# Two 128-row loads of a gated linear-attention kernel issued as two 64-row halves each

## The chip, the cores and the metric

The kernel runs on one core of a Trainium2 chip. The metric is the device time of one execution in microseconds (us); several executions are given, and their median is used. The engines are named as in the profile: PE is TensorE (its matmuls), PEld its weight loads, DVE is VectorE, ACT is ScalarE, POOL is GpSimd and SP is SyncE, which here only issues DMAs. ACT issues DMAs as well. In the profile the DMA queue q1 holds what SP issues, and q10 what ACT issues.

## The reference

```python
def _A_ref(x, wqkv, wo):            # B = 1, S = 2048, D = 640, bfloat16
    B, S, D = x.shape
    H = 32; Dh = D // H             # 32 heads of 20
    qkv = (x @ wqkv).reshape(B, S, 3, H, Dh).transpose(2, 0, 3, 1, 4)
    q, k, v = qkv[0], qkv[1], qkv[2]
    phi = lambda t: jnp.where(t > 0, t + 1, jnp.exp(t)) + 1e-6
    pq, pk = phi(q), phi(k)
    kv = jnp.einsum("bhsd,bhse->bhde", pk, v)
    z = jnp.einsum("bhsd->bhd", pk)
    num = jnp.einsum("bhqd,bhde->bhqe", pq, kv)
    den = jnp.einsum("bhqd,bhd->bhq", pq, z)[..., None] + 1e-6
    return (num / den).transpose(0, 2, 1, 3).reshape(B, S, D) @ wo
# _B_ref: the same with B's weights
x = A_x
g = sigmoid((x * gate_w).sum(-1, keepdims=True))
return g * _A_ref(x, A_wqkv, A_wo) + (1 - g) * _B_ref(x, B_wqkv, B_wo)
```

Both branches read the same `x`; only the weights differ.

## The kernel before

The 2048 rows of `x` are 16 tiles of 128 rows, the 640 features are 5 chunks of 128. All operations go through a small scheduler of the program (`sch.op`): each operation names what it reads and writes by keys such as `("XN", 0)`, and the scheduler puts in semaphore waits. It does not reorder: every engine runs its operations in the order in which the program names them.

The part that the change touches is the front, the first few microseconds. `XN` holds rows of `x` as they lie in memory, `XT` holds `x` transposed, and `WKT` holds the K weights, chunk by chunk (A's chunk `c` has the key `("WKH", 0, c)`). Every DMA is made by the helper `dma` (line 315), which gives it a semaphore of its own. The order of the front is written out by hand:

- SP's queue: `load_xn` for tiles 0, 1, 2, 3 of `x` (128 rows of 1280 bytes, 160 KB each), then A's K weights chunk 4, then B's K weights (two DMAs), then 15 DMA transposes that bring `XT` for tiles 4 to 15, then all the other loads.
- ACT's queue: `load_wk` for A's K weights chunks 0, 1, 2, 3 (160 KB each), then the gate's weights (`GWR`). These stand behind an exponential of one element (line 428) that brings in ACT's function table, and ahead of ACT's first work on data.
- PE: `fill` runs matmuls of a constant into a bank that nobody reads; `turn(t)` transposes tile `t` of `x` on PE, five transposes of 128x128 against the identity `IDN` (line 487), which DVE and ACT then copy to `XT` (lines 501 and 499); `ks((t, c))` is the part of the K projection of tile `t` for chunk `c`, one 512-wide and one 128-wide matmul.

PE's order at the front is

```python
fill(4, 12, 256)        # line 1037: 12 matmuls, 256 wide
turn(0, early)
fill(4, 1, 128)
ks((0, 0))
turn(1, early)
ks((0, 1), (1, 0), (1, 1))
turn(2, late)
ks((0, 2), (1, 2), (2, 0), (2, 1), (2, 2))
```

and then the gate's weights (`GWR`), tile 3, the rest of the K projection of tiles 0 to 3 for A, the same tiles for B, and pairs of both for tiles 4 to 15. Behind that come the Q projections, the per-head sums, and the output, in all some 180 us in which PE hardly pauses.

Of the kernel before, what the change touches and what calls it, by code (L numbers as in the profile page):

```python
# [8 lines left out]
ACT = mybir.ActivationFunctionType  # L9
# [3 lines left out]
D = 640  # L13
# [4 lines left out]
NC = 5  # L18
# [202 lines left out]
def bass_gated_mix__linear_attn_block__linear_attn_block__prompt_kernel(  # L221
# [16 lines left out]
    wqkv = {"A": A_wqkv, "B": B_wqkv}  # L238
    wo = {"A": A_wo, "B": B_wo}
    BR = ("A", "B")  # L240

    with ExitStack() as es:
        E = es.enter_context

        def sb(name, shape, dtype=dt.bfloat16):
            return E(nc.sbuf_tensor(name, shape, dtype))
# [3 lines left out]
        IDN = sb("IDN", [128, 128])  # L250
        GWR = sb("GWR", [128, 128])
        XN = sb("XN", [128, NT, D])
        XT = sb("XT", [128, NC, S])
# [4 lines left out]
        WKT = sb("WKT", [128, NC, BLO + 512])  # L258
# [5 lines left out]
        PK = {X: PKT[:, i, :, :] for i, X in enumerate(BR)}  # L264
# [29 lines left out]
        def bank(i, lo, hi, p0=0, p1=128):  # L294
            o = 512 * (i % 2)
            return PP[i // 2][p0:p1, o + lo : o + hi]
# [4 lines left out]
        def new_sem(name):  # L301
            n_sem[0] += 1
            return E(nc.semaphore(name="d%d_%s" % (n_sem[0], name)))

        sch = _Sched()

        def dma(eng, name, o_ap, i_ap, reads=(), writes=(), transpose=False, noncontig=None):
            sem = new_sem(name)

            def fn(engobj):  # L310
                if noncontig is not None:
                    with nc.allow_non_contiguous_dma(reason=noncontig):
                        ins = engobj.dma_start(o_ap, i_ap, transpose=transpose)
                else:
                    ins = engobj.dma_start(o_ap, i_ap, transpose=transpose)
                return ins.then_inc(sem, 16)

            return sch.op(eng, fn, reads=reads, writes=writes, name=name, sem=sem, total=16)

        def mms(steps, reads=(), writes=(), name=""):  # L320


            def fn(pe):
                ins = None
                for o, l, r, st, sp, tp in steps:
                    ins = pe.matmul(o, l, r, start=st, stop=sp, tile_position=tp)  # L326
                return ins

            return sch.op("PE", fn, reads=reads, writes=writes, name=name)
# [5 lines left out]
        def act(fn, reads=(), writes=(), name=""):  # L335
            return sch.op("ACT", fn, reads=reads, writes=writes, name=name)

        def dve(fn, reads=(), writes=(), name=""):
            return sch.op("DVE", fn, reads=reads, writes=writes, name=name)
# [4 lines left out]
        xin = A_x[0]  # L344


        def load_xn(eng, t0, t1):
            dma(
                eng,
                "xn%d" % t0,  # L350
                XN[:, t0:t1, :],
                xin[128 * t0 : 128 * t1, :].rearrange("(t p) f -> p t f", p=128),
                writes=[("XN", t) for t in range(t0, t1)],
            )
# [32 lines left out]
        def wk(X, c, h):  # L387

            if X == "A":
                return WKT[:, c, 512:D] if h else WKT[:, c, 0:512]  # L390
            return WKT[:, c, BHI : BHI + 129] if h else WKT[:, c, BLO : BLO + 512]

        def wk_reads(X):

            return [("WKH", BR.index(X), c) for c in range(NC)] + ([("WKL", c) for c in range(NC)] if X == "B" else [])

        def load_wk(eng, X, c0, c1):
            w = wqkv[X][128 * c0 : 128 * c1, D : 2 * D].rearrange("(c p) f -> p c f", p=128)
            parts = ((0, 0, D, "WKH"),) if X == "A" else ((BLO, 0, 512, "WKL"), (BHI, 512, D, "WKH"))
            for o, lo, hi, key in parts:  # L400
                dma(
                    eng,
                    "wk%s%d" % (X, c0),
                    WKT[:, c0:c1, o : o + hi - lo],
                    w[:, :, lo:hi],
                    writes=[(key, c) if key == "WKL" else (key, BR.index(X), c) for c in range(c0, c1)],
                )
# [10 lines left out]
                fill=0.0,  # L418
            ),
            reads=[("ONE",)],  # L420
            writes=[("IDN",)],
        )
        pool(lambda e: e.memset(GWR[:, :], 0.0), writes=[("GWZ",)])
        for X in BR:
# [3 lines left out]
            lambda e: e.activation(SG[:, 2, 0:1], nc.const_aps.tensor(1.0, (128, 1), dt.float32), ACT.Exp),  # L428
            writes=[("SGE", 0)],
        )  # L430
        for t in range(4):
            load_xn("SP", t, t + 1)
            load_wk("ACT", "A", t, t + 1)

# [5 lines left out]
            reads=[("GWZ",)],  # L440
            writes=[("GWR",)],
# [3 lines left out]
        for b in range(1, NB):  # L445
            for c in range(NC):
# [5 lines left out]
                    writes=[("XT", t, c) for t in range(4 * b, 4 * b + 4)],  # L452
# [19 lines left out]
        def fill(bk, n, w=512):  # L472
            mms(
                [(bank(bk, 0, w), C1[:, 0:128], C1[:, 0:w], True, True, None)] * n,
                writes=[("PS", bk)],
                name="fill",
            )

        def turn(t, parts):
            for cs, bk in parts:  # L480
                n = len(cs)
                dst = bank(bk, 0, 64 * n).bitcast(dt.bfloat16)

                def tr(pe, dst=dst, cs=cs):
                    ins = None
                    for i, c in enumerate(cs):
                        ins = pe.transpose(  # L487
                            dst[:, 128 * i : 128 * i + 128],
                            XN[:, t, 128 * c : 128 * c + 128],
                            IDN[:, :],  # L490
                        )
                    return ins

                sch.op("PE", tr, reads=[("XN", t), ("IDN",)], writes=[("PS", bk)], name="tr%d" % t)
                o = XT[:, cs[0] : cs[0] + n, 128 * t : 128 * t + 128]
                i = dst.rearrange("p (c s) -> p c s", c=n)
                ks = [("XT", t, c) for c in cs]
                if cs[-1] == NC - 1:
                    act(lambda e, o=o, i=i: e.activation(o, i, ACT.Copy), reads=[("PS", bk)], writes=ks)
                else:  # L500
                    dve(lambda e, o=o, i=i: e.tensor_copy(o, i), reads=[("PS", bk)], writes=ks)  # L501
# [4 lines left out]
        def k_part(X, t, pp, cs, first, last):  # L506
            P = PP[pp]
            xs = slice(128 * t, 128 * t + 128)
            bks = [("PS", 2 * pp), ("PS", 2 * pp + 1)]
            for c in cs:  # L510
                l = XT[:, c, xs]
                st, sp = first and c == cs[0], last and c == cs[-1]
                mms(
                    [
                        (P[:, 0:512], l, wk(X, c, 0), st, sp, None),
                        (P[:, 512:D], l, wk(X, c, 1), st, sp, None),
                    ],
                    reads=[("XT", t, c), ("WKH", 0, c)],
                    writes=bks,
                    name="k%s%d" % (X, t),  # L520
                )
# [130 lines left out]
        def g_run(X, j, pp, units, out=()):  # L652


            P = PP[pp]
            steps = []
            for t, h in units:
                o, r = (
                    (P[:, 0:512], PK[X][:, t, 0:512]),
                    (P[:, 512:D], PK[X][:, t, 512:D]),  # L660
                    (P[:, 512 : D + 128].rearrange("p (i f) -> p i f", i=2), PKT[:, :, t, 512:D]),
                )[h]
                steps.append((o, XN[:, t, 128 * j : 128 * j + 128], r, t == 0, t == NT - 1, None))
            ts = sorted({t for t, h in units})
            two = any(u[1] == 2 for u in units)
            mms(
                steps,
                reads=[("XN", t) for t in ts] + [("PK", Y, t) for t in ts for Y in (BR if two else X)],
                writes=[("PS", 2 * pp + h) for h in (0, 1) if any((u[1] > 0) == h for u in units)],
                name="g%s%d" % (X, j),  # L670
            )
            for lo, hi, o, key in out:
                act(
                    lambda e, lo=lo, hi=hi, o=o: e.activation(o, P[:, lo:hi], ACT.Copy),  # L674
                    reads=[("PS", 2 * pp + h) for h in (0, 1) if (hi > 512 if h else lo < 512)],
                    writes=[(key, j)],
                )
# [352 lines left out]
        def ks(*units):  # L1030
# [3 lines left out]

        early = (((0,), 6), ((1, 2), 7), ((3, 4), 5))
        late = (((0, 1, 2), 6), ((3, 4), 7))
        fill(4, 12, 256)
        turn(0, early)
        fill(4, 1, 128)
        ks((0, 0))  # L1040
# [6 lines left out]
            reads=[("GWR",), ("GWZ",), ("IDN",)],  # L1047
            writes=[("PS", 7)],
            name="gw",
# [4 lines left out]
            reads=[("PS", 7)],  # L1054
            writes=[("GW",)],
# [76 lines left out]
        for i, fn in enumerate(late):  # L1132
            fn()
            if i % 4 == 3 and groups:
                X, b = groups.pop(0)
# [72 lines left out]
```

## Time and profile before

| what | value |
|---|---|
| median of 3 runs | 190.44 us (190.39 to 190.78) |
| the profiled execution | 190.54 us |
| its span, first to last instruction | 189.3 us |
| what lies around the span | 1.2 us |
| PE busy | 186.5 us, 99% of the span |
| DVE busy | 121.1 us, 64% |
| ACT busy | 69.2 us, 37% |
| DMA, mean over the span | 121 GB/s |

The span is the time from the first to the last instruction of one profiled execution; the time of that execution also has a start and an end that no instruction shows. Starts in the views are microseconds from the span's start. Matmuls are pipelined and their ends are modelled: of a row of matmuls the distance between starts tells the pace, not the length of one. Idle time is put in brackets behind an instruction, with what ended it.

### The profile page before, as it was taken

How to read it: one execution, taken by the hardware profiler on the slowest of the kernel's cores; microseconds unless marked ns; L12 is line 12 of the kernel's file. 1: busy time of each engine (PE TensorE's matmuls, PEld its weight loads, DVE VectorE, ACT ScalarE, POOL GpSimd, SP SyncE). 2: the span in 40 equal slices, each digit the busy share in tenths (PEclk: the TensorE clock that was granted, in tenths of full speed). 3: DMA queues.
4: the chain of work that ended last, by engine and by line, in shares of the span. 5: the costliest groups of instructions: out<-in, count | busy, mean ns of one | idle time of the engine just before them, and what ended most of it. 6: DMA issues, size and time to landing. Idle time of an engine off the chain costs nothing.

```text
span 189.3 us, 3423 instructions
## 1 busy us (share of the span) xinstructions
PE 186.5 (99%) x1310; PEld 101.4 (54%) x1310; DVE 121.1 (64%) x223; ACT 69.2 (37%) x137; POOL 45.7 (24%) x49
## 2 busy tenths in 40 slices
PE   8999999999999999999999999999999999999995
PEld 5655555555545455455455555744447555555554
DVE  1289999999997756565565665495035961976223
ACT  3276565666544442532532632270214500000000
POOL 2000323223244746635645543000000000000000
PEclk9999999999999999999999999999999999999999
DMA  5965459998493501261000003206586599321212
GB/s 180 342 128 88 100 97 187 359 281 178 143 282 44 5 0 13 90 146 38 0 3 3 0 2 101 74 3 166 178 249 186 170 228 311 114 84 55 73 69 69
DMA packets 38946, 22.91 MB, mean 121 GB/s; under 512 B 24090, under 2 KB 37394, under 8 KB 38930
## 3 DMA queue, kind: packets, MB, share of 16 engines
q1 hardware_dynamic: 36136, 19.62, 40.1%
q10 hardware_dynamic: 2794, 3.08, 5.4%
q8 instruction: 10, 0.16, 0.4%
q14 instruction: 6, 0.05, 0.1%
HBM read 16.78 MB, written 3.95 MB: 109 GB/s over the span
## 4 chain that ended last, share of the span: by engine, by line
PE 99%; DVE 0%; issue 0%
PE ps L326 98%; PE ps L487 1%; DVE OSTG L1010 0%
## 5 line engine op out<-in xcount | busy, mean ns | idle before, releaser
L694 POOL TENSOR_TENSOR ZS<-ZS,PKT 128x640 f32<-128x640 f32 x26 | 37.6, 1445 | 43.2 <-DVE PKT L602 20.6
L326 PE MATMUL ps<-PKT,XN 128*128 128x512 bf16 (+2 forms) x256 | 46.7, 332 | 0.0
L326 PE MATMUL ps<-WKT,XT 128*128 128x512 bf16 (+3 forms) x260 | 44.9, 334 | 0.0
L627 ACT ACTIVATE EQ<-ps 128x512 bf16<-128x512 f32 x40 | 23.9, 598 | 35.8 <-PE ps L326 35.4
L326 PEld LDWEIGHTS ps<-PKT,XN 128*128 128x128 bf16 x256 | 23.8, 98 | 21.6 <-ACT GT L674 0.2
L326 PEld LDWEIGHTS ps<-WKT,XT 128*128 128x128 bf16 x260 | 24.0, 99 | 19.6 <-DVE XT L501 0.3
L632 DVE TENSOR_SCALAR EQ<-EQ 128x512 bf16<-128x512 bf16 x40 | 15.0, 375 | 21.2 <-ACT EQ L627 20.4
L326 PE MATMUL ps<-WPA,PQA 128*128 128x512 bf16 (+4 forms) x165 | 26.3, 295 | 0.0
L326 PE MATMUL ps<-WPB,PQB 128*128 128x512 bf16 (+4 forms) x165 | 26.0, 295 | 0.0
L326 PE MATMUL ps<-XT,WQB 128*128 128x512 bf16 x100 | 23.2, 379 | 0.0
L326 PE MATMUL ps<-XT,WQA 128*128 128x512 bf16 x100 | 23.1, 379 | 0.0
L586 ACT ACTIVATE EK<-ps 128x512 bf16<-128x512 f32 (+1 forms) x36 | 18.4, 527 | 11.3 <-PE ps L326 9.9
L602 DVE SCALAR_TENSOR_TENSOR PKT<-ps,EK 128x512 bf16<-128x512 f32 (+1 forms) x36 | 21.7, 603 | 1.2
L326 PEld LDWEIGHTS ps<-WPA,PQA 128*128 128x128 bf16 x165 | 13.4, 98 | 9.4
L326 PEld LDWEIGHTS ps<-WPB,PQB 128*128 128x128 bf16 x165 | 13.3, 98 | 9.0
L1010 DVE CAST OSTG<-ps 128x640 bf16<-128x640 f32 (+2 forms) x13 | 9.6, 751 | 11.6 <-PE ps L326 11.6
L326 PEld LDWEIGHTS ps<-XT,WQB 128*128 128x128 bf16 x100 | 9.7, 98 | 10.6
L326 PEld LDWEIGHTS ps<-XT,WQA 128*128 128x128 bf16 x100 | 9.6, 98 | 10.7
L637 DVE SCALAR_TENSOR_TENSOR PQA<-ps,EQ 128x512 bf16<-128x512 f32 x20 | 13.8, 692 | 0.7
L637 DVE SCALAR_TENSOR_TENSOR PQB<-ps,EQ 128x512 bf16<-128x512 f32 x20 | 13.8, 692 | 0.7
L1012 ACT ACTIVATE OSTG<-ps 128x256 bf16<-128x256 f32 x1 | 0.4, 385 | 37.0 <-PE ps L326 37.0
L674 ACT ACTIVATE GT<-ps 128x640 bf16<-128x640 f32 (+1 forms) x10 | 6.5, 652 | 17.9 <-PE ps L326 17.9
(67 smaller groups left out, 105.5 us busy)
## 6 DMA issues: line engine op xcount, KB each, us to landing
out_dram<-OSTG SPq DMA_DIRECT2D x15, 160.0 KB, 1.8
XN<-in_A_x_dram SPq DMA_DIRECT2D x3, 640.0 KB, 7.8
WKT<-in_A_wo_dram SPq DMA_DIRECT2D x8, 160.0 KB, 4.5
PKT<-rsA SPq DMA_DIRECT2D x10, 128.0 KB, 3.4
XT<-rsB ACTq DMA_DIRECT2D x8, 128.0 KB, 5.6
WVA<-in_A_wqkv_dram SPq DMA_DIRECT2D x1, 800.0 KB, 9.9
WVB<-in_B_wqkv_dram SPq DMA_DIRECT2D x1, 800.0 KB, 5.4
XN<-in_A_x_dram SPq DMA_DIRECT2D x4, 160.0 KB, 3.3
```

The costliest lines, as they stand in the source:

```text
L326: ins = pe.matmul(o, l, r, start=st, stop=sp, tile_position=tp)
L487: ins = pe.transpose(dst[:, 128 * i : 128 * i + 128], XN[:, t, 128 * c : 128 * c + 128], IDN[:, :],)
L586: lambda e, ek=ek, ps=ps: e.activation(ek, ps, ACT.Exp),
L602: lambda e, o=o, v=v, ek=ek, ps=ps: e.scalar_tensor_tensor(out=o, in0=v(ps), scalar=0.0, in1=v(ek), op0=ALU.max, op1=ALU.add),
L627: lambda e: e.activation(EQ[:, slot, :], bank(bk, 0, 512), ACT.Exp),
L632: lambda e: e.tensor_scalar(EQ[:, slot, :], EQ[:, slot, :], 1.0, EPS, op0=ALU.min, op1=ALU.add),
L637: lambda e: e.scalar_tensor_tensor(out=PQ[X][:, k, cols], in0=bank(bk, 0, 512), scalar=0.0, in1=EQ[:, slot, :], op0=ALU.max, op1=ALU.add,),
L674: lambda e, lo=lo, hi=hi, o=o: e.activation(o, P[:, lo:hi], ACT.Copy),
L694: lambda e: e.tensor_tensor(out=ZS[:, :], in0=a, in1=b, op=ALU.add),
L1010: dve(lambda e, o=o, p=p: e.tensor_copy(o, p), reads=bks, writes=keys)
L1012: act(lambda e, o=o, p=p: e.activation(o, p, ACT.Copy), reads=bks, writes=keys)
```

## The change

Tile 0 of `x` and chunk 0 of A's K weights are each loaded by two DMAs of 64 rows instead of one of 128. The first 64 rows of each go through SP's queue, the others through ACT's queue; on both queues the half tile of `x` stands ahead of the half chunk of weights. Behind them SP loads tiles 1 to 3 of `x` as before and ACT chunks 1 to 3 of the weights. So each queue has one DMA more ahead of what follows. The first halves get keys of their own (`("XN", 0, "a")`, `("WKH", 0, 0, "a")`), and the readers of tile 0 and chunk 0 name both keys. At the front PE runs 10 instead of 12 of the 256-wide constant matmuls. The engines' orders are otherwise the same.

```diff
-        for t in range(4):
+        for o, src, key in (
+            (XN[:, 0, :], xin[0:128, :], ("XN", 0)),
+            (WKT[:, 0, 0:D], wqkv["A"][0:128, D : 2 * D], ("WKH", 0, 0)),
+        ):
+            for i, eng in enumerate(("SP", "ACT")):
+                r = slice(64 * i, 64 * i + 64)
+                dma(eng, "h%s%d" % (key[0], i), o[r, :], src[r, :], writes=[key] if i else [key + ("a",)])
+        for t in range(1, 4):
             load_xn("SP", t, t + 1)
             load_wk("ACT", "A", t, t + 1)
...
-                sch.op("PE", tr, reads=[("XN", t), ("IDN",)], writes=[("PS", bk)], name="tr%d" % t)
+                sch.op("PE", tr, reads=[("XN", t), ("XN", t, "a"), ("IDN",)], writes=[("PS", bk)], name="tr%d" % t)
...
-                    reads=[("XT", t, c), ("WKH", 0, c)],
+                    reads=[("XT", t, c), ("WKH", 0, c), ("WKH", 0, c, "a")],
...
-        fill(4, 12, 256)
+        fill(4, 10, 256)
```

More of the change, by code (lines that the diff above doesn't have):

```diff
@@ L393, in wk_reads @@
         def wk_reads(X):
-            return [("WKH", BR.index(X), c) for c in range(NC)] + ([("WKL", c) for c in range(NC)] if X == "B" else [])
+            return [("WKH", BR.index(X), c) for c in range(NC)] + [("WKH", 0, 0, "a")] + ([("WKL", c) for c in range(NC)] if X == "B" else [])
         def load_wk(eng, X, c0, c1):
@@ L667, in g_run @@
                 steps,
-                reads=[("XN", t) for t in ts] + [("PK", Y, t) for t in ts for Y in (BR if two else X)],
+                reads=[("XN", t) for t in ts] + [("XN", 0, "a")] + [("PK", Y, t) for t in ts for Y in (BR if two else X)],
                 writes=[("PS", 2 * pp + h) for h in (0, 1) if any((u[1] > 0) == h for u in units)],
```

## The prediction

> **What bounds the kernel now.** I read the page's busy times and chain first, then the front of the span as a timeline, then the DMAs of the same stretch by queue. The page says that PE is the bound from end to end:
>
> ```profile
> PE 186.5 (99%) x1310; PEld 101.4 (54%) x1310; DVE 121.1 (64%) x223; ACT 69.2 (37%) x137; POOL 45.7 (24%) x49
> ...
> PE 99%; DVE 0%; issue 0%
> ```
>
> So the change is worth what it moves in PE's stream at the front. The timeline of PE and its weight loads there:
>
> ```profile
> 0.84 2.72 PE L326 MATMUL ps<-const-bfloat16-1.0 128*128 128x256 bf16 x12 [0.84 <-PEq L1193]
> 3.58 0.45 PEld L487 LDWEIGHTS ps<-IDN,XN 128*128 128x128 bf16 x5 [0.50 <-DMA XN<-in_A_x_dram]
> 3.59 0.71 PE L487 MATMUL ps<-IDN,XN 128*128 128x128 bf16 x5
> 4.20 0.74 PE L326 MATMUL ps<-WKT,XT 128*128 128x512 bf16 x2
> 4.73 0.74 PE L487 MATMUL ps<-IDN,XN 128*128 128x128 bf16 x5
> 5.27 1.57 PE L326 MATMUL ps<-WKT,XT 128*128 128x512 bf16 x6
> 6.67 0.44 PE L487 MATMUL ps<-IDN,XN 128*128 128x128 bf16 x5
> 6.95 1.52 PE L326 MATMUL ps<-WKT,XT 128*128 128x512 bf16 x10
> ```
>
> Three things stand there. First, the real work begins at 3.59, when tile 0 of x has landed, and from then on every group begins where the one before it leaves the array. Second, the fills are over a little earlier: two that straddle 3.2 start at 2.93 and end (modelled) at 3.57, so they start 0.21 us apart, and twelve of them leave the array at 0.84 + 12 x 0.21 = 3.35. PE is short of work for about 0.24 us, no more. Third, the pace doubles inside the six matmuls at 5.27. A pair of 512 and 128 wide takes 4.73 - 4.20 = 0.53 us before them and (8.31 - 6.95)/5 = 0.27 us behind them (8.31 is where the next group begins). The six take 6.67 - 5.27 = 1.40 us; with n slow pairs, 0.53n + 0.27(3 - n) = 1.40, n = 2.2, and the step lies at about 6.45. The clock column of the profile reads 1.00 throughout and does not show this, so I go by the spacing. What PE does before 6.45 takes twice its time: work that starts d earlier there brings the end forward by d/2 only.
>
> Then the DMAs, between 2.55 and 2.90 and between 2.90 and 3.30:
>
> ```profile
> DMA packets 98, 0.13 MB, mean 358 GB/s; under 512 B 0, under 2 KB 98, under 8 KB 98
> ...
> q1 hardware_dynamic: 98, 0.13, 100.2%
> ```
>
> ```profile
> DMA packets 136, 0.15 MB, mean 384 GB/s; under 512 B 16, under 2 KB 136, under 8 KB 136
> ...
> q10 hardware_dynamic: 104, 0.13, 89.4%
> q1 hardware_dynamic: 32, 0.02, 16.0%
> ```
>
> Between 1.8 and 2.55 only 14 packets moved, all on q1. Then q1 alone has all 16 engines (tile 0 of x), then q10 has them (chunk 0 of the weights), then q1 again (tile 1). The two queues take turns, and x already goes first, at full rate. Its landing is 0.81 + 2.7 = 3.5.
>
> **The change part by part.** The sum is against the profiled execution, 190.54 us (span 189.3 and 1.2 around it), which lies 0.10 above the median of 190.44; at the end I take the 0.10 off.
>
> *Tile 0 in two halves.* It is the same 160 KB on the same 16 engines. At 384 GB/s that is 0.42 us, before as one turn of q1, now as half a turn of q1 and half a turn of q10. What precedes is a start, not a transfer: from the issue at 0.81 to 2.55 hardly anything moves. The halves are issued at 0.81 (SP) and 0.87 (ACT, where the weights' first DMA stands now), so both are in the queues long before 2.55. I take the landing unchanged at 3.5. Bounds: if q10 does not start as early as q1, the nearest row is its first packets at about 2.9, behind which half a tile needs 0.21 us, so tile 0 is whole some 0.15 us later; if the start-up is shared out and vanishes, the tile could come up to 2.55 - 1.84 = 0.7 us earlier (1.84: 0.81 plus the 1.03 us to the first packet). In PE's time that is +0.08 to -0.35 us; I take 0.
>
> A rule of the Trainium skill speaks against this part. DMA: Bandwidth & Descriptors, section Rules for kernel authors, says that two transfers to disjoint halves of the partitions share the same 16 engines, so splitting brings nothing and one transfer of 128 partitions is better. The full rate on q1 alone agrees with it; by the rule this term is 0 or a small loss, against the -0.35 of the other bound.
>
> *Ten fills instead of twelve.* They leave the array at 0.84 + 10 x 0.21 = 2.94, so 0.43 us of constant work goes. Nothing reads it, and tile 0 is not there yet: the idle time ahead of the transposes grows from 0.24 to 0.65 us. That costs 0, covered by the wait for tile 0. If that cover is gone, because the tile lands earlier, the fills' removal is what lets PE use it.
>
> *Two more DMA issues, and what they are moved past.* On SP the issues stand 0.46 us apart, so tiles 1, 2, 3, chunk 4, B's weights and the 15 transposes are all issued some 0.46 later. Tile 1 would be issued at 1.73 instead of 1.27; its data moved from about 3.3, and before that the queues are busy with tile 0 and chunk 0 in either version. It landed at 1.27 + 3.1 = 4.4 and is used at 4.73: 0.3 us in hand. Tile 2 (used at 6.67) and what follows have over 1 us in hand, B's weights too (landed 3.6 + 5.9 = 9.5; A's 22 K matmuls from 8.6 on, 0.27 a pair, last until 11.6). The DMA transposes are first needed by tile 4 at about 17, and the loads behind them later still. On ACT the same 0.46 moves the gate's weights (landed 6.8, used at 8.3) and ends the issuing at about 3.8 instead of 3.3; ACT's first copy starts at 4.34, so that is hidden too. Sum 0; the upper bound, if tile 1 came the whole 0.46 late, is a stall of 0.15 us.
>
> *More waits.* The first transpose and the first K matmul each wait for one semaphore more. A separate wait takes PE's queue about 0.05 us. The K matmul's lie ahead of its wait for DVE's copy and are hidden; the transpose's can show where both halves land together: 0 to 0.05 us, half of it in the end. I take 0.02.
>
> Sum: 190.54 + 0 + 0 + 0 + 0.02 = 190.56, less 0.10: **190.45 us** for the median, no change. What a measurement of this kernel can tell from no change is about 0.2%, 0.38 us.
>
> **The rivals.**
>
> *The clock steps up later (slower).* PE's pace doubled at 6.45, after 2.9 us of unbroken real work, and behind a front that had only 0.24 us of idle time in it. With 0.65 us idle the front is thinner, and if whatever counts PE's activity finds the stretch too thin, the doubling comes one stretch later. It decides at the point where the idle time counts as a break; the trace shows that 0.24 does not, and nothing about 0.65. The price: a stretch as long as the one from 3.59 (2.9 us) or from the end of the fills at 2.94 (3.5 us), at half pace, costs 1.4 to 1.75 us, so 191.9 to 192.2. For it: the fills have no other purpose, and the change takes two away. Against it: 0.65 us is a small part of 5.6 us of cold time. Chance 0.28. The Trainium skill (TensorE: Matmul & The Clock Gate, Part 1) has this as a rule: the clock doubles after one busy window of about 3.4 us, which runs freely. By its figure a window missed would cost an estimate of 1.7 us; how busy a window must be it does not say. That the windows run freely is not what the three runs show, which lie within 0.39 us.
>
> *The start-up shrinks (faster).* If two queues get through the start faster, tile 0 lands up to 0.7 us earlier and everything behind it with it, PE starts at 2.95 and the fills have no gap behind them. That is 0.64/2 = 0.32 us: 190.1. If the doubling also moves with the work, again 0.32: 189.8. The 1.7 us from issue to 2.55 speak for something to be won; that those rows show only q1 at that time and no queueing behind it speaks against. With half of it won, 190.3, it is inside the 0.2%. Chance over the bound 0.12.
>
> *The second slots come late (slower).* Tile 0 is whole only with the later half, and tile 1 stands in the third slot instead of the second. 0.08 + 0.15 + 0.02 is 0.25: 190.7, inside the bound; with a later start of ACT's queue it passes it. Chance over the bound 0.07.
>
> **How the numbers follow.** No change, with the small parts of the second and third rival, 0.53; clock late 0.28 and late slots 0.07 make slower 0.35; faster 0.12. The likeliest time is 190.45, its own range 190.1 to 190.7. The whole range reaches up to the late clock, 192.2, and leaves out most of the faster case.
>
> **What would show it.** Right: the first transposes again at about 3.6 behind some 0.65 us of idle time, q1 and q10 sharing the engines from 2.55, the doubling at about 6.45, and all later starts within 0.1 us. Wrong: five transposes of tile 2 with 0.107 us between starts (late clock; the group then lasts about 0.74 instead of 0.44), a first transpose at or before 3.3 (shrunken start-up), or a stall ahead of tile 1's transposes (late slots).

## The result and the profile after

The changed kernel is slower: 1.0072 times the kernel before, 95% interval 1.0048 to 1.0096. That is 0.0072 x 190.4 = 1.4 us. Over nine executions each, the medians are 192.32 us (191.00 to 193.93) and 190.39 us (189.94 to 190.78), which is 1.9 us. The ratios, here and below, leave out executions of more than 1.5% above the fastest of their kernel, two of the changed kernel (193.92 and 193.93) and three of `e10_x_columns`, although the clock reads 1.00 in them too. The scatter is itself a result: 2.9 us against 0.8.

The execution that was profiled is the fastest of the nine, 191.00 us (span 189.7). Its busy times and its chain:

```profile
PE 185.4 (98%) x1308; PEld 100.6 (53%) x1308; DVE 121.2 (64%) x223; ACT 69.0 (36%) x137; POOL 45.8 (24%) x49
...
PE 96%; DMA 2%; ACTq 0%; ACT 0%; DVE 0%; issue 0%
PE ps L326 95%; DMA WKT<-in_A_wqkv_dram 2%; ACTq L315 0%; ACT L428 0%; PE ps L495 0%; DVE OSTG L1018 0%; ACT SG L428 0%
```

A load of `WKT` now holds 2% of the chain, which was PE alone before. The timeline of PE's matmuls at the front shows which one:

```profile
0.84 2.29 PE L326 MATMUL ps<-const-bfloat16-1.0 128*128 128x256 bf16 x10 [0.84 <-PEq L1201]
...
3.55 0.71 PE L495 MATMUL ps<-IDN,XN 128*128 128x128 bf16 x5 [0.42 <-DMA XN<-in_A_x_dram]
...
5.27 0.43 PE L326 MATMUL ps<-WKT,XT 128*128 128x512 bf16 x2 [0.92 <-DMA WKT<-in_A_wqkv_dram]
...
5.54 0.44 PE L495 MATMUL ps<-IDN,XN 128*128 128x128 bf16 x5
...
6.17 0.99 PE L326 MATMUL ps<-WKT,XT 128*128 128x512 bf16 x6 [0.19 <-DMA WKT<-in_A_wqkv_dram]
```

Tile 0's transposes start at 3.55, as before. The first K matmul starts at 5.27 instead of 4.20, because chunk 0 of the weights, now in two halves, landed at 5.0 and 5.2 instead of 3.9. The pace had doubled by then, in this execution: tile 1's transposes take 0.44 us, not 0.74. In a second profile of the same loads (the run `e2_fill12` below, 192.92 us) the wait is longer and the doubling comes only at about 9.8. How the 1.4 us of all the executions divide between waiting and a late doubling is therefore not read from this one profile.

The issues on both queues until 3.2:

```profile
0.80 0.57 SPq L315 DMA_DIRECT2D XN<-in_A_x_dram  x1
1.43 0.57 SPq L315 DMA_DIRECT2D WKT<-in_A_wqkv_dram  x1
2.05 1.53 SPq L315 DMA_DIRECT2D XN<-in_A_x_dram  x3
```
```profile
0.86 0.59 ACTq L315 DMA_DIRECT2D XN<-in_A_x_dram  x1
1.48 0.80 ACTq L315 DMA_DIRECT2D WKT<-in_A_wqkv_dram  x1
```

An issue of 64 rows takes 0.57 to 0.80 us. Before, four issues of 128 rows on SP took 1.82 us together. So chunk 0 is issued at 1.43 and 1.48 instead of 0.87, and tile 1 at 2.05 instead of 1.27. Last, what the DMA engines moved, first in the kernel before and then in the changed one (last column GB/s):

```profile
1.50:2.60 1.10, 1.10 (x7) 0.79 (x6) 0.00 (x0) 0.79 (x2) 0.24 (x5) 1.00 0.37 27
2.60:4.60 2.00, 1.97 (x12) 1.07 (x11) 0.51 (x2) 0.26 (x1) 0.00 (x0) 1.00 1.05 385
4.60:6.60 2.00, 2.00 (x12) 1.31 (x11) 0.51 (x2) 0.51 (x2) 0.00 (x0) 1.00 1.07 372
```
```profile
1.50:2.60 1.10, 1.10 (x7) 0.77 (x6) 0.00 (x0) 0.78 (x2) 0.24 (x5) 1.00 0.33 78
2.60:4.60 2.00, 1.33 (x9) 0.60 (x7) 0.50 (x2) 0.05 (x1) 0.00 (x0) 1.00 0.88 243
4.60:6.60 2.00, 1.14 (x10) 0.71 (x11) 0.42 (x2) 0.71 (x2) 0.00 (x0) 1.00 1.00 300
```

The engines were at 385 GB/s from 2.6 on and are at 243 now, though their busy share fell only from 1.05 to 0.88. Between 2.9 and 3.3, where q10 had 104 packets and q1 had 32, there are now:

```profile
DMA packets 51, 0.06 MB, mean 144 GB/s; under 512 B 6, under 2 KB 51, under 8 KB 51
...
q1 hardware_dynamic: 37, 0.04, 70.5%
q10 hardware_dynamic: 14, 0.01, 14.5%
```

There are 51 packets instead of 136, for a busy share of 85% instead of 105% (the sums over both queues): single packets take long. A packet of 1280 bytes mostly takes 55 ns. Of the packets that start in the span's first 8.5 us, eight take over 0.4 us in the trace of before, and all of them start between 1.84 and 2.16; in the changed kernel there are ten, the first at 3.15, the last at 6.38. The long packets that stood ahead of tile 0 stand behind it now.

From the first 257-wide matmul (tile 4 of the K projection) on, all is as it was: from its start to the start of the last matmul it takes 167.94 us in both profiles. All of the difference arises ahead of it.

### The profile page after: what moved, and what is told of

It is laid out like the page before. It is cut to its first block, busy times and chain, and to the rows that moved or that the text cites. A ratio compares the mean times of both kernels' runs of the same rounds, so it can differ in the third digit from the quotient of the medians.

```text
span 189.7 us, 3421 instructions
## 1 busy us (share of the span) xinstructions
PE 185.4 (98%) x1308; PEld 100.6 (53%) x1308; DVE 121.2 (64%) x223; ACT 69.0 (36%) x137; POOL 45.8 (24%) x49
## 4 chain that ended last, share of the span: by engine, by line
PE 96%; DMA 2%; ACTq 0%; ACT 0%; DVE 0%; issue 0%
PE ps L326 95%; DMA WKT<-in_A_wqkv_dram 2%; ACTq L315 0%; ACT L428 0%; PE ps L495 0%; DVE OSTG L1018 0%; ACT SG L428 0%
## 5 line engine op out<-in xcount | busy, mean ns | idle before, releaser
L326 PE MATMUL ps<-WKT,XT 128*128 128x512 bf16 (+3 forms) x260 | 44.1, 330 | 1.1 <-DMA WKT<-in_A_wqkv_dram 1.1
```

## The experiments

Two theories stood after this. **Late data**: chunk 0 and what follows land late, and PE waits. **Late clock**: idle holes at the front put off the doubling of PE's pace. Times are medians, ratios are against the kernel before on the same chip, with their 95% intervals.

**e1_fill10: fewer fills alone.**

```diff
-        fill(4, 12, 256)        # the kernel before
+        fill(4, 10, 256)
```


> The kernel before with 10 instead of 12 wide fills, loads untouched. Late-data theory (the halves and what follows them land late, and the first K matmul waits for them): the fills cover a wait, so 190.4, within 0.2 of before; first transposes at about 3.6, first K matmul at about 4.2. Late-clock theory (the thinner front makes PE's pace double a stretch later): 191.5 to 192.2, and transposes of tile 2 still 0.107 us apart.

190.68 us, 1.0013 (0.9996 to 1.0030). The two fills cost nothing that can be told. The profile has the same loads as before, yet its 11 packets of over 0.4 us start between 2.2 and 5.6; tile 0 and chunk 0 landed at 3.6 and 3.9, and PE never waited behind tile 0's transposes. So packets that come late are not peculiar to split loads; here they did not hit what PE needed next.

**e2_fill12: the fills back, the split loads kept.**

```diff
-        fill(4, 10, 256)        # the changed kernel
+        fill(4, 12, 256)
```


> The changed kernel with the 12 fills of before. Late-data theory: the first K matmul still waits until about 5.2, and the time stays with the changed kernel, 191.5 to 192.5. Late-clock theory: the front is as full as before, 190.4 to 191.

191.86 us, 1.0079 (1.0055 to 1.0102): as the changed kernel. From its timeline:

```profile
5.66 0.69 PE L326 MATMUL ps<-WKT,XT 128*128 128x512 bf16 x2 [1.40 <-DMA WKT<-in_A_wqkv_dram]
6.14 0.74 PE L495 MATMUL ps<-IDN,XN 128*128 128x128 bf16 x5
...
8.27 0.74 PE L495 MATMUL ps<-IDN,XN 128*128 128x128 bf16 x5
8.81 2.00 PE L326 MATMUL ps<-WKT,XT 128*128 128x512 bf16 x10
```

Tile 2's transposes still take 0.74 us at 8.27. The ten matmuls last until 10.65, 1.84 us for five pairs, so n pairs at 0.53 and the others at 0.27 give n = 1.9: the doubling comes at about 9.8. Late data and a late clock stand in the same profile, which is that of the longest of the six executions.

**e3_same_queue: split, but not shared out.**

```diff
-        for o, src, key in (                              # the changed kernel
-            (XN[:, 0, :], xin[0:128, :], ("XN", 0)),
-            (WKT[:, 0, 0:D], wqkv["A"][0:128, D : 2 * D], ("WKH", 0, 0)),
+        for o, src, key, eng in (
+            (XN[:, 0, :], xin[0:128, :], ("XN", 0), "SP"),
+            (WKT[:, 0, 0:D], wqkv["A"][0:128, D : 2 * D], ("WKH", 0, 0), "ACT"),
         ):
-            for i, eng in enumerate(("SP", "ACT")):
+            for i in (0, 1):
```


> Both halves of the tile of x on SP's queue, both halves of the weights on ACT's; 10 fills; each queue still has one DMA more ahead of what follows. If it is the sharing of one tile over two queues that lands it late: chunk 0 is in by about 4.0 as before, and 190.4 to 190.8. If it is the additional issue slot on each queue, or the small transfers themselves: as the changed kernel, chunk 0 in at about 5, 191.5 to 192.5.

192.20 us, 1.0107 (1.0072 to 1.0141). The second half of x stands behind a 0.58 us issue and lands at 4.6:

```profile
4.66 0.71 PE L495 MATMUL ps<-IDN,XN 128*128 128x128 bf16 x5 [1.53 <-DMA XN<-in_A_x_dram]
```

Keeping each split load on one queue does not take the loss away, so the sharing is not needed for it; but the loss falls elsewhere, ahead of tile 0 instead of behind it.

**e4_x_halves and e8_w_halves: one of the two loads split.**

```diff
-            (WKT[:, 0, 0:D], wqkv["A"][0:128, D : 2 * D], ("WKH", 0, 0)),   # e4: x halves only
...
+        load_wk("ACT", "A", 0, 1)
```
```diff
+        load_xn("SP", 0, 1)                                                 # e8: weight halves only
         for o, src, key in (
-            (XN[:, 0, :], xin[0:128, :], ("XN", 0)),
```


> Only the tile of x is split over the queues; chunk 0 of the weights is one DMA of 128 rows on ACT's queue behind the second half of x; 10 fills. SP's queue has no additional issue, ACT's has one. If the splitting over two queues costs per split transfer: chunk 0 in at about 4.2 to 4.5, 190.8 to 191.4. If the additional slots cost: SP's side as before, ACT's weights 0.5 us late, 190.6 to 191. If any split lets the queues run into each other for good: as the changed kernel, 191.5 to 192.5.

> Tile 0 of x whole and first on SP's queue; only chunk 0 of the weights is split, its first half second on SP, its other half first on ACT; 10 fills. If a 64-row DMA at the head makes its queue's issues long: ACT's issues take 0.58 us, SP's 0.40, the half on SP lands by 4.3 and the time is 190.7 to 191.4. If the splitting as such costs: chunk 0 in at about 5, 191.5 to 192.5.

193.60 us, 1.0160 (1.0124 to 1.0196), and 191.59 us, 1.0081 (1.0051 to 1.0112). Neither half of the change is the harmless one. e4 lies above everything that was expected of it, and its median above the changed kernel's; why one split load costs more than two was not found. With the weights alone split, the queue that starts with 128 rows issues those in 0.39 us, and the 64-row DMA behind it takes 0.56:

```profile
0.80 0.39 SPq L315 DMA_DIRECT2D XN<-in_A_x_dram  x1
...
1.25 0.56 SPq L315 DMA_DIRECT2D WKT<-in_A_wqkv_dram  x1
```

The 64-row DMA is long wherever it stands. In e4 the whole chunk, second on ACT behind a 64-row half, takes 0.83 us to issue and lands at 5.2:

```profile
1.45 0.83 ACTq L315 DMA_DIRECT2D WKT<-in_A_wqkv_dram  x1
```

**e7_columns: halves by columns.** The 64-row shape goes, the additional slot stays.

```diff
-                r = slice(64 * i, 64 * i + 64)            # the changed kernel
-                dma(..., o[r, :], src[r, :], ...)
+                r = slice(320 * i, 320 * i + 320)
+                dma(..., o[:, r], src[:, r], ...)
```


> The changed kernel with halves of 320 columns of all 128 rows instead of halves of 64 rows: as many DMAs in the same order on the same queues. If the 64-row shape makes the issues long (0.58 us instead of 0.40): issues of 0.40 to 0.45 us, chunk 0 in by 4.0 to 4.4, 190.5 to 191. If one DMA more at the head of each queue is what costs: issues of 0.45 to 0.6 us and chunk 0 in at 4.8 to 5.3, 191.5 to 192.5.

192.51 us, 1.0116 (1.0094 to 1.0138). The issues take 0.38 to 0.45 us, and both first loads land early, x at 3.1 and chunk 0 at 3.8:

```profile
3.17 0.71 PE L495 MATMUL ps<-IDN,XN 128*128 128x128 bf16 x5
...
3.86 0.69 PE L326 MATMUL ps<-WKT,XT 128*128 128x512 bf16 x2
5.66 0.71 PE L495 MATMUL ps<-IDN,XN 128*128 128x128 bf16 x5 [1.10 <-DMA XN<-in_A_x_dram]
6.16 1.81 PE L326 MATMUL ps<-WKT,XT 128*128 128x512 bf16 x6
```

PE starts 0.4 us earlier and waits 1.1 us for tile 1, which was issued at 1.72 and lands at 5.6. The doubling comes at about 8.7. The issues and chunk 0 are as the first case expected, the time is as the second. So the long issues may explain why it was chunk 0 that came late, but not that something comes late. The rate between 2.6 and 4.6 is as in the changed kernel:

```profile
2.60:4.60 2.00, 1.91 (x11) 0.75 (x9) 0.51 (x2) 0.39 (x1) 0.00 (x0) 1.00 0.97 242
```

**e9_small_first: one small DMA ahead on each queue, nothing split.**

```diff
+        for i, eng in enumerate(("SP", "ACT")):           # the kernel before
+            dma(eng, "t%d" % i, OSTG[:, i, 0:64], xin[0:128, 64 * i : 64 * i + 64], ...)
         for t in range(4):
```


> The kernel before with one small DMA (128 rows of 128 bytes of x, into an output buffer that is written only much later) at the head of each queue; tile 0 and chunk 0 are whole again and stand second, 12 fills. If one DMA more at the head of each queue is enough (the packets of 0.4 us and more then fall on later transfers, as in the runs with split loads): tile 0 in at 3.7 to 4.3, long packets spread over 3 to 8 us, 191 to 192.5. If splitting is needed for that and the slot costs only its 0.46 us: tile 0 in at 3.5 to 4.0, long packets only before 2.7 us, 190.4 to 190.9.

190.86 us, 1.0030 (1.0004 to 1.0056). Tile 0 lands at 4.1, half a microsecond late, and the long packets spread from 2.4 to 7.4. Every queue has its additional slot, as in the changed kernel, and it costs 0.6 us in the middle, less than half of the changed kernel's 1.4. Its packets are as the first case expected, its time as the second. In this profile the pace had doubled by 4.12, ahead of the first transposes.

**e10_x_columns: x by columns, the weights whole.**

```diff
-            (WKT[:, 0, 0:D], wqkv["A"][0:128, D : 2 * D], ("WKH", 0, 0)),   # e7_columns
...
+        load_wk("ACT", "A", 0, 1)
```


> Only tile 0 of x is split, by columns (128 rows of 320 columns on each queue); chunk 0 of the weights is one DMA, second on ACT's queue; 10 fills. SP has no additional slot. If the long packets are what costs, wherever a split puts them: tile 0 in at 3.1 to 3.3, then a wait of 1 us or more ahead of the first K matmul or of tile 1, 191.3 to 192.5. If the 64-row halves' long issues and the additional slot on SP were the cost: tile 0 in at 3.2, chunk 0 by 4.0, tile 1 by 4.4, 190.1 to 190.5.

192.45 us (190.50 to 195.19), 1.0071 (1.0040 to 1.0102). SP has no additional slot and no long issue here, tile 1 landed at 4.05, and the gain of 0.4 us at tile 0 is lost all the same: the first K matmul starts at 4.53, and the next weights hold PE up for 1.67 us more in the execution that was profiled, which is one of its long ones (194.31):

```profile
4.53 0.69 PE L326 MATMUL ps<-WKT,XT 128*128 128x512 bf16 x2 [0.49 <-DMA WKT<-in_A_wqkv_dram]
...
7.43 1.78 PE L326 MATMUL ps<-WKT,XT 128*128 128x512 bf16 x6 [1.67 <-DMA WKT<-in_A_wqkv_dram]
```

**e6_one_fill: a hole in front, data as before.**

```diff
-        fill(4, 12, 256)        # the kernel before
+        fill(4, 1, 256)
```


> The kernel before with 1 instead of 12 wide fills; PE is idle from about 1.1 to 3.6. If PE's activity sets when the pace doubles: the doubling comes 1.5 to 3 us later than in the kernel before, 191.2 to 192. If idle time has no part in it: 190.4, as before.

191.95 us, 1.0076 (1.0054 to 1.0098), the changed kernel's loss with the loads of before. The rate is 377 GB/s from 2.6 to 4.6, and nothing waits behind tile 0:

```profile
3.71 0.72 PE L487 MATMUL ps<-IDN,XN 128*128 128x128 bf16 x5 [2.50 <-DMA XN<-in_A_x_dram]
4.22 0.31 PE L326 MATMUL ps<-const-bfloat16-1.0 128*128 128x128 bf16 x1
4.33 0.74 PE L326 MATMUL ps<-WKT,XT 128*128 128x512 bf16 x2
...
6.99 0.74 PE L487 MATMUL ps<-IDN,XN 128*128 128x128 bf16 x5
7.53 1.74 PE L326 MATMUL ps<-WKT,XT 128*128 128x512 bf16 x10
```

PE's work starts 0.12 us later than before; the rest is pace, which doubles at about 8.0 instead of 6.45. This shows the late clock by itself.

**e5_bridge: the changed kernel with its holes filled.**

```diff
-        fill(4, 10, 256)        # the changed kernel
+        fill(4, 13, 256)
         turn(0, early)
-        fill(4, 1, 128)
+        fill(4, 12, 128)
```


> The changed kernel with constant matmuls in its two holes: 13 wide fills ahead of tile 0's transposes, and 12 instead of 1 of the 128-wide ones ahead of the first K matmul. They do no useful work; the data land as in the changed kernel. If PE's pace doubles late because PE sat idle in the holes: the doubling comes by 6.5 to 7.5 and the time is 191.0 to 191.6, with less scatter than the changed kernel. If only the waiting counts and the doubling comes at a time of its own: no gain, 191.9 to 192.5, and the scatter stays.

191.50 us (191.14 to 191.73), 1.0058 (1.0042 to 1.0075). The data are as late as ever, the first K matmul starts at 5.38, and the pace doubles within tile 1's transposes, at about 6.1; one wait for weights is left behind them, 0.37 us at 7.92:

```profile
5.38 0.74 PE L326 MATMUL ps<-WKT,XT 128*128 128x512 bf16 x2
5.91 0.54 PE L495 MATMUL ps<-IDN,XN 128*128 128x128 bf16 x5
6.29 0.98 PE L326 MATMUL ps<-WKT,XT 128*128 128x512 bf16 x6
```

The scatter shrinks from 2.9 us (nine executions) to 0.6 (six). The ratio's interval overlaps the changed kernel's, so how much of the median the filling buys is not settled; that the long executions vanish with the holes fits the late clock.

**e11_fill13: one fill more.**

```diff
-        fill(4, 12, 256)        # the kernel before
+        fill(4, 13, 256)
```


> The kernel before with 13 instead of 12 wide fills, so that the last of them ends where tile 0 lands. If idle time ahead of the doubling costs in proportion (1 fill was 1.5 us slower, 10 were 0.15 us): 190.2 to 190.4, at most 0.1% faster. If only a hole of a microsecond or more counts: as before, within 0.1%. If tile 0 often lands before 3.6: up to 0.1 us slower.

190.55 us, 1.0001 (0.9981 to 1.0021): no difference. In the profiled execution the pace doubles as early as about 4.2, and then PE waits 0.67 us for tile 2 at 6.57. In this execution the early doubling gains little, since tile 2 lands only at 6.5:

```profile
4.22 0.45 PE L326 MATMUL ps<-WKT,XT 128*128 128x512 bf16 x2
...
6.57 0.45 PE L487 MATMUL ps<-IDN,XN 128*128 128x128 bf16 x5 [0.67 <-DMA XN<-in_A_x_dram]
```

No version that was run beats the kernel before.

**The terms side by side**, from the traces. "Waits" are what starts lie apart beyond the pace, where that is over 0.1 us, between the first transposes and the first 257-wide matmul; the idle times in brackets, which go by modelled ends, come to less (1.11, 1.40 and 1.10 us in the last three rows). "Slow" is what the matmuls in that stretch took over their full-pace time:

| profile | first transposes | waits | slow | first 257-wide matmul |
|---|---|---|---|---|
| before | 3.59 | 0 | 1.29 | 19.21 |
| e6_one_fill | 3.71 | 0 | 2.02 | 20.00 |
| changed | 3.55 | 1.51 | 0.20 | 19.64 |
| e2_fill12 | 3.43 | 1.61 | 2.28 | 21.55 |
| e7_columns | 3.17 | 1.31 | 1.97 | 20.74 |

The last column is the sum of the three before it and some 14.3 us of work at full pace. The changed kernel and e2_fill12 have the same loads; their 0.43 and 2.34 us over before lie on both sides of the 1.4 us that the ratio gives.

## Why the prediction was right or wrong

The likeliest case, no change at 190.45, was wrong. By the ratio the time is 1.0072 x 190.44 = 191.8, inside the range that reached up to 192.2; the plain median, 192.32, is just above it. That the range reached so far is in part luck: its upper end was the price of a clock put off by the missing fills, and the missing fills cost nothing that can be told.

- **Tile 0 in two halves**, taken as 0: right for tile 0. Its transposes start at 3.55 against 3.59, 0.05 us behind the landing in both, so the term *More waits* does not show either. The rule of the Trainium skill (DMA: Bandwidth & Descriptors, Rules for kernel authors) that halves of a tile are not worth two DMAs holds here: the loss is 1.4 us. The "start-up shrinks" rival was half there: with column halves tile 0 landed 0.4 us earlier. But the pause was paid behind tile 0, in the transfers that PE needs next. That the stream behind it would stay at full rate was the unspoken part, and it failed: 243 GB/s for 385.
- **Two more DMA issues**, taken as 0: the step that failed. It followed tile 1, tile 2, B's weights and the transposes, and left out the transfer that the change moves most. Chunk 0 goes from the first slot of ACT's queue to the second slot of both. It landed at 3.9 and was used at 4.2, 0.3 us in hand; it now lands at 5.2. Chunk 1, landed at 4.8 and used at 5.27 before, is not in the list either; it now lands at 6.1. The spacing of 0.46 us was wrong too: at 0.62 to 0.84 us the second slots are issued later than reckoned, by 0.16 on SP, and the third by 0.3 on SP and 0.5 on ACT. The spacing alone does not explain the loss: in e7 it is as reckoned and chunk 0 is in time, and yet tile 1, issued 0.45 us later, lands 1.2 us later. What failed there is the reckoning that a later issue moves a landing by no more than itself.
- **Ten fills instead of twelve**, taken as 0: right (1.0013 when done alone).
- **The clock steps up later**: the mechanism is real and its price of 1.4 to 1.75 us about right, but its place was wrong. The 0.65 us ahead of the transposes cost nothing that can be told (e1_fill10); a hole of 2.5 us costs 0.0076 x 190.4 = 1.4 us (e6_one_fill), and with the changed kernel's loads the hole is the wait for chunk 0, 1.1 us and more, which the forecast did not have. Of the two profiles with these loads and this hole, e2_fill12 shows the doubling put off; in the changed kernel's own the pace had doubled by 5.27, across the hole.
- **"That the windows run freely is not what the three runs show"** was wrong. Without large holes the doubling came at about 6.45, 7.2, 6.1 and 4.2 (before, e1, e5, e11), up to 3.0 us apart, and by 4.12 in e9. That the runs of before lie close together all the same may be because an early doubling runs into data that are not there, as in the one profile of e11; this is not shown. TensorE: Matmul & The Clock Gate, Part 1, of the Trainium skill has a freely running window of about 3.4 us; these spreads agree with it, but none of these runs was made to test it.
- **The second slots come late**, priced at 0.25 us: the right kind of delay, the wrong transfers and the wrong size. It named tile 0 and tile 1; in the profile PE waits for chunk 0 and then for chunk 1 of the weights, and the waits measure 1.5 us.

## What to carry to other kernels

When one DMA becomes two, list every transfer that changes its slot, the moved one first, and compare each with the moment of its first use; a margin of 0.3 us did not survive a slot here. Look also at where the long packets at the start of the DMA stream fall: ahead of the first transfer they are covered by the fills, on a transfer that PE needs next they are a wait. While PE runs at half pace, a wait can cost twice: its own length, and the chance that it puts off the doubling.

## What had not been expected of the hardware

- A DMA of 64 rows of 1280 bytes took longer to issue (0.56 to 0.83 us) than one of 128 rows (0.38 to 0.45), and the whole DMAs close behind it were slow too (0.56 to 0.83). Why is open. The issues of 0.80 us and more are all the second on ACT's queue and end at 2.28 to 2.29, as ACT's exponential does (2.29), so a part of their length may be that.
- The first packet of the program's loads started at 2.16 in the five profiles in which both queues begin with 64 rows, and at 1.81 to 1.84 in the other eight.
- Every profile has some 6 to 17 packets of 0.4 to 1.5 us in the first 8.5 us. With the loads of before they fall together ahead of tile 0 in two profiles of four, and partly later in the others; behind split loads most come after 2.7. What holds these packets up was not found.
- The clock column of the profile reads 1.00 while PE runs at half pace, in every profile of this case. The spacing of starts (0.107 against 0.056 us for 128 columns) tells it.
